# Seeding two of five accumulation banks by ScalarE in a fused attention and gate kernel

## The chip, the cores and the metric

The kernel runs on one core of a Trainium2 chip. The metric is the device time of one execution in microseconds (us), the median of several runs. Its engines are TensorE (PE, with its weight loads shown as PEld), VectorE (DVE), ScalarE (ACT), GpSimd (POOL) and SyncE (SP, which here issues loads and stores). Each engine works through its own instructions in the order in which they stand; semaphores hold an instruction back until another engine's result is there.

## The reference, cut to what matters

```python
xn = layernorm(x)                                  # x: 2048 rows of 640
q = (xn @ wq) as 32 heads of 128                   # k, v: the last 512 rows of the caches
p = softmax(q @ k.T * 128 ** -0.5)                 # for each head: 2048 x 512
s = concat(p @ v for the 32 heads) @ wo            # 2048 x 4096 times 4096 x 640
g = silu(relu(xn @ w1 + b1) ** 2 @ w2 + b2)        # 640 -> 1728 -> 640
return x + s * g
```

The output projection `@ wo` sums over all 32 heads. That running sum is what the change touches.

## The kernel before, in words

**Precision.** All products are float32. Each operand is split into a high part, which TensorE's float32r format holds, and the rest; `triple` (L560) then makes three products, high by high, high by low, low by high, into one PSUM bank. So one logical 128x128 by 128x512 product is three PE matmuls and three weight loads.

**Stages.** A first stage (to about 315 us of the trace) normalizes the rows and computes the gate for three of the four 512-row tiles. The attention stage follows and takes nearly all the rest; a short tail computes the last tile's gate and the final products.

**Units.** The attention stage is cut into 128 units (L540): two halves of the rows, in each half 16 groups of two heads, in each group two row tiles of 512, for each tile the two heads. Unit i is one head on one row tile. Each unit gets a period of nominally 12.4 us in a plan that is written out by hand (`at`, `on`, the loop from L1050): every step has a due time, the steps are sorted by it, and each engine gets its instructions in that order. The due times fix only the order.

**One unit's steps**, spread over several periods: `q_mm` (15 matmuls into a PSUM bank), `q_hi` on ACT and `q_lo` on DVE split the result and empty the bank; `s_mm` makes the scores in four banks (12 matmuls); `max_fold` on DVE takes maxima (4 instructions, tile `rdm`), `gather` on ACT and `row` on DVE finish them, and two DMAs spread them over the partitions; `shift` on DVE (4 instructions, tile `e`), `expo`, `p_hi` on ACT and `p_lo`, `s_add` on POOL make the weights; `s_fold` on DVE, `gather` on ACT (tile `rds`) and `row` sum them; `v_mm` multiplies by v (12 matmuls, tile `o`); `o_norm` on DVE, `o_hi` on ACT, `o_lo` on DVE scale and split the result (tile `ot`). `prep` splits the next heads' weights: a copy on ACT (tiles `wq`, `wk`, `wv`, `wo`) and a subtraction on POOL, two such pairs in most periods.

**The output projection.** After each second unit (odd i) the two heads' results are multiplied by their rows of `wo`, for five blocks d = 0 to 4 of 128 output columns: `r_mm` (L739), six matmuls a block, into bank `r`. `r_acc` (L753) then adds the bank to the running sum `ACC` (tile `acc`, in SBUF): in a half's first group (g == 0) ACT copies the bank there, in all later groups DVE adds it with one `tensor_tensor`.

**The two banks.** The tags `qr0` and `qr1` (`bank`, L566) are shared by `q_mm` (always `qr1`) and the five blocks (`R_BANK`, L1049: blocks 0 and 3 in `qr1`; 1, 2 and 4 in `qr0`). A bank's next user waits until the last one has been read out.

**The order on PE.** By `R_AT` (L1038), for a pair of odd unit i: in the period of an odd unit p, PE runs the scores of p (12), the second half of block 2 of unit p-4 (3), the queries of p+2 (15), **block 4 of unit p-4** (6), the products with v of p-1 (12), **block 0 of unit p-2** (6). In an even unit's period it runs scores (12), block 1 (6), queries (15), the first half of block 2 (3), v (12) and block 3 (6). So each pair of periods has 108 matmuls and all five blocks once.

**Instruction placement.** `align` (L1035) fills PE's instruction stream with no-operations up to fixed places, so that each period's instructions start at a multiple of 128. Between the last scores and the next period stand 42 matmuls with their 42 weight loads, from place 42 on, which leaves two places.

Of the kernel before, what the change touches and what calls it, by code (L numbers as in the profile page):

```python
# [10 lines left out]
AF = mybir.ActivationFunctionType  # L11
# [14 lines left out]
def kernel(  # L26
# [42 lines left out]
    class Ordered:  # L69
# [13 lines left out]
    pe, dve, act, pool, sp = (  # L83
        Ordered(e) for e in (nc.tensor, nc.vector, nc.scalar, nc.gpsimd, nc.sync)
    )
# [8 lines left out]
    def raw(ap):  # L94
        return ap.bitcast(F32)
# [387 lines left out]
    def mlp_step(n):  # L483
# [56 lines left out]
    units = [  # L540
        (hf, g, t, g * G + j)
        for hf in range(HALF)
        for g in range(NG)
        for t in range(TPH)
        for j in range(G)
    ]
    NU = len(units)
    UPG = TPH * G
    PERIOD = 12.4
    B32 = 32  # L550
    AHEAD = 2
    NQ = NT // B32
    NH = KC // 2

    XT, ACC, KT, VV, WQ, WO, Q, E, SC, MB, RD, PT, PO, OT, RB, QPS, FX, CL, PRS, RAW = (
        {} for _ in range(20)
    )
    pools = {}

    def triple(ps, a, b, start, stop):  # L560
        (ah, al), (bh, bl) = a, b
        pe.matmul(ps, ah, bh, start=start, stop=False)
        pe.matmul(ps, ah, bl, start=False, stop=False)
        pe.matmul(ps, al, bh, start=False, stop=stop)

    def bank(name, k):  # L566
        return pools["psa"].tile([P, NT], F32, tag=f"qr{k}", name=name, bufs=1)
# [19 lines left out]
    def pair(tag, shape, name, bufs):  # L587
        return [
            pools["ep"].tile(shape, F32R, tag=f"{tag}{i}", name=f"{name}_{i}", bufs=bufs)
            for i in range(2)  # L590
        ]
# [17 lines left out]
    def q_mm(i, cs):  # L609
        hf, g, t, h = units[i]  # L610
        if 0 in cs:
            QPS[i] = bank(f"pq{i}", 1)
        ws, xs = WQ[hf, h], XT[hf, t]
        for c in cs:
            triple(
                QPS[i],
                (ws[0][:, c, :], ws[1][:, c, :]),
                (xs[0][:, c, :], xs[1][:, c, :]),
                c == 0,
                c == DC - 1,  # L620
            )

    def q_hi(i):
        Q[i] = pair("q", [P, NT], f"q{i}", AHEAD + 1)
        act.activation(Q[i][0], QPS[i], AF.Copy, scale=SCALE)
# [6 lines left out]
    def s_mm(i, c):  # L632
        hf, g, t, h = units[i]
        SC[i, c] = pools["psb"].tile([P, NT], F32, tag="s", name=f"s{i}_{c}", bufs=KC)
        ks = KT[hf, h]
        cs = slice(c * P, (c + 1) * P)
        triple(SC[i, c], (ks[0][:, cs], ks[1][:, cs]), Q[i], True, True)

    def fold_tile(what, i):
        n = KC if what == "m" else 2  # L640
        return ap.tile([P, NQ, P // B32, n], F32, tag=f"rd{what}", name=f"rd{what}{i}", bufs=2)

# [16 lines left out]
    def row(i, what):  # L659
        rd = RD.pop((i, what))[:B32].rearrange("p b a c -> p b (a c)")  # L660
        r = ap.tile([B32, B32], F32, tag="row", name=f"row{what}{i}", bufs=4)
        if what == "m":
            r = r[:, :NQ]
            dve.tensor_reduce(r, rd, axis=AX.X, op=ALU.max)
        else:
            sq = SQ[i % len(SQ)]
            dve.tensor_reduce(sq[:, :NQ], rd, axis=AX.X, op=ALU.add)
            dve.reciprocal(sq[:, :NQ], sq[:, :NQ])
            dve.transpose(r, sq)
            r = r[:NQ]  # L670
        d = dpool.tile(list(r.shape), F32, tag=f"{what}_d", name=f"{what}_d{i}", bufs=4)
# [40 lines left out]
    def v_mm(i, c):  # L712
        hf, g, t, h = units[i]
        if c == 0:
            if i % 2 or i < UPG:
                PO[i] = pools["psb"].tile([P, NT], F32, tag="o", name=f"o{i}", bufs=1)
            else:
                PO[i] = psx.tile([P, NT], F32, tag="x", name=f"o{i}")
        vs, pts = VV[hf, h], PT[i, c // 2]
        triple(  # L720
            PO[i],
            (vs[0][:, c, :], vs[1][:, c, :]),
            (pts[0][:, c % 2, :], pts[1][:, c % 2, :]),
            c == 0,
            c == KC - 1,
        )
# [9 lines left out]
    def o_lo(i):  # L736
        dve.tensor_tensor(OT[i][1], PO.pop(i), raw(OT[i][0]), op=ALU.subtract)

    def r_mm(i, d, js, k):  # L739
        hf, g, t, h = units[i]  # L740
        if 0 in js:
            PRS[i, d] = bank(f"r{i}_{d}", k)
        for j in js:
            w = WO[hf, h - G + 1 + j]
            triple(
                PRS[i, d],
                tuple(x[:, d * P : (d + 1) * P] for x in w),
                tuple(OT[i - G + 1 + j]),
                j == 0,
                j == G - 1,  # L750
            )

    def r_acc(i, d):  # L753
        hf, g, t, h = units[i]
        pr = PRS.pop((i, d))
        if g == 0:
            if d == 0:
                ACC[hf, t] = keep.tile(
                    [P, DC, NT], F32, tag="acc", name=f"acc{hf}_{t}", bufs=TPH
                )  # L760
            act.activation(ACC[hf, t][:, d, :], pr, AF.Copy)
        else:
            a = ACC[hf, t][:, d, :]
            dve.tensor_tensor(a, pr, a, op=ALU.add)
# [139 lines left out]
    def late_split(f):  # L904
        n = chunks[f][1]
        r = LR.pop(f)
        kind, bufs = ("wk", G) if f % 2 else ("q", AHEAD + 1)
        if n < P:
# [93 lines left out]
    def at(when, f, *a):  # L1002
        plan.append((max(when, 0.0), len(plan), f, a))

    for n in range(HALF * NG):
        hf, g = divmod(n, NG)
        base = UPG * PERIOD * n
        for j in range(G):
            h = g * G + j
            for kind, when in (  # L1010
                ("q", (j - 1 - AHEAD) * PERIOD + (8.42 if j else 8.35)),
                ("k", (j - 2) * PERIOD + (8.5 if j else 8.37)),
# [36 lines left out]
    R_BANK, R_BANK_END = (1, 0, 0, 1, 0), (1, 1, 1, 0, 0)  # L1049
    for i in range(NU):  # L1050
        t0 = i * PERIOD

        def on(when, f, *a):
            at(t0 + when, f, *a)

        hf, g, t, h = units[i]
        for c in range(KC):
            on(0.68 * c, align, i, SLOTS[c])
            on(0.68 * c, s_mm, i, c)
        on(0.68 * KC - 0.6, align, i, SLOTS[KC])  # L1060
        qs = [(i + AHEAD, 3.45 if i % G and i > UPG else 4.3, 4.1)]
        if i == 0:
            qs = [(1, 2.8, 4.1), (2, 9.1, PERIOD - 5.2)]
        elif i < UPG:
            qs = [(i + 2, 4.9 if i == 3 else 4.2, 4.1)]
        for n, q_at, low in qs if i + AHEAD < NU else ():
            for c in range(DC):
                on(q_at + 0.68 * c, q_mm, n, (c,))
            on(q_at + 3.5, q_hi, n)
            on(q_at + low, q_lo, n)  # L1070
        for c in range(KC):
            on(0.8 + 0.68 * c, max_fold, i, c)
        on(3.95, gather, i, "m")
        on(4.1, row, i, "m")
        for c in range(KC):
            on(10.4 + 0.4 * c, shift, i, c)
        on(11.7, expo, i, 0)
        on(12.7, p_hi, i, 0)
        on(13.8, expo, i, 1)
        on(PERIOD + 4.0, p_hi, i, 1)  # L1080
        on(13.9, p_lo, i, 0)
        on(16.2, s_add, i)
        on(PERIOD + 6.2, s_fold, i)
        on(PERIOD + 8.0, gather, i, "s")
        on(PERIOD + 8.5, row, i, "s")
        on(18.6, p_lo, i, 1)
        for c in range(KC):
            on(PERIOD + 8.5 + 0.68 * c, v_mm, i, c)
        on(2 * PERIOD + 4.2, o_norm, i)
        on(2 * PERIOD + 4.9, o_hi, i)  # L1090
        on(2 * PERIOD + 5.5, o_lo, i)
        if i % G == G - 1:
            for d in range(DC):
                last = i == NU - G - 1
                if i < NU - 1:
                    for when, js in (R_AT_END if last else R_AT)[d]:
                        on(when, r_mm, i, d, js, (R_BANK_END if last else R_BANK)[d])
                    on(when + 0.68 * len(js), r_acc, i, d)
                if g == NG - 1 and hf == 0:
                    at((i + (3, 4, 5, 4, 5)[d] + (t and d in (0, 3, 4))) * PERIOD + 4.3, store_acc, t, d)  # L1100
                    w = (NU // 2 + 9 + 4 * (t * DC + d)) * PERIOD
                    for k, n in enumerate("sxg"):
                        at(w + k * PERIOD - 0.6, load_finish, n, 0, t, d)
                    at(w + 3 * PERIOD - 0.7, finish_gate, 0, t, d)
                    at(w + 3 * PERIOD - 0.7, finish, 0, t, d)
# [49 lines left out]
    for f, u in sorted(UP_AT.items()):  # L1155
        at(LOAD.get(f, PREP.get(f - 2, 0) + 0.9), late_load, 1, f)
        when = PREP.setdefault(f, u - 5.0)
# [85 lines left out]
```

## Time and profile before

| what | value |
| --- | --- |
| median of 3 runs | 1958.74 us (1958.74 to 1959.13) |
| span of the profiled execution, first to last instruction | 1956.9 us |
| PE busy | 1949.2 us, 8612 matmuls |
| DVE busy | 1537.3 us |
| POOL busy | 1376.7 us |
| ACT busy | 1187.6 us |

The profile is of one execution. Its span leaves out what lies around the instructions: the median of the timed runs is 1.8 us more. A timeline row reads: start in us from the span's start, the time that the group took, engine, source line, operation, out<-in by the program's names, shape, number of instructions that were merged into the row, and in brackets the engine's idle time before it with what ended it. Nearly all attention instructions carry line 77, because a helper there issues them; they are told apart by their tiles. `r` is a block of the output projection, `acc` the running sum, `pq` the queries' bank, `s` the scores, `o` the products with v.

### The profile page before, as it was taken

How to read it: one execution, taken by the hardware profiler on the slowest of the kernel's cores; microseconds unless marked ns; L12 is line 12 of the kernel's file. 1: busy time of each engine (PE TensorE's matmuls, PEld its weight loads, DVE VectorE, ACT ScalarE, POOL GpSimd, SP SyncE). 2: the span in 40 equal slices, each digit the busy share in tenths (PEclk: the TensorE clock that was granted, in tenths of full speed). 3: DMA queues.
4: the chain of work that ended last, by engine and by line, in shares of the span. 5: the costliest groups of instructions: out<-in, count | busy, mean ns of one | idle time of the engine just before them, and what ended most of it. 6: DMA issues, size and time to landing. Idle time of an engine off the chain costs nothing.

```text
span 1956.9 us, 28182 instructions
## 1 busy us (share of the span) xinstructions
PE 1949.2 (100%) x8612; PEld 1612.5 (82%) x8612; DVE 1537.3 (79%) x2638; ACT 1187.6 (61%) x2040; POOL 1376.7 (70%) x757
## 2 busy tenths in 40 slices
PE   9999999999999999999999999999999999999998
PEld 7888888888888888888888888888888888888887
DVE  6523337788888888888888878888888888888865
ACT  5432336766666666666666676666666666666643
POOL 2121226888888888888888888888888888888841
PEclk9999999999999999999999999999999999999999
DMA  6330454333333332332335434433333333332353
GB/s 189 88 119 28 185 198 130 97 94 92 93 92 93 92 92 92 92 92 93 93 91 179 141 117 109 114 114 114 114 113 114 113 114 114 98 92 92 85 189 118
DMA packets 127892, 219.13 MB, mean 112 GB/s; under 512 B 23452, under 2 KB 38086, under 8 KB 126470
## 3 DMA queue, kind: packets, MB, share of 16 engines
q1 hardware_dynamic: 124742, 202.75, 34.3%
q0 software_dynamic: 2864, 14.42, 1.8%
q8 instruction: 77, 1.26, 0.2%
q14 instruction: 65, 0.53, 0.1%
q10 hardware_dynamic: 144, 0.16, 0.0%
HBM read 193.41 MB, written 23.87 MB: 111 GB/s over the span
## 4 chain that ended last, share of the span: by engine, by line
PE 99%; DVE 0%; DMA 0%; ACT 0%; issue 0%; POOL 0%; POOLq 0%
PE pq L77 22%; PE r L77 22%; PE o L77 18%; PE s L77 18%; PE ph L431 7%; PE ly L77 2%; PE py L101 2%; PE py L100 2%; PE py L102 2%; PE lu L77 2%; PE eu L77 1%; PE ph L398 0%; PE py L454 0%; PE py L453 0%; DMA xb<-in_x_dram 0%; PE px L77 0%
## 5 line engine op out<-in xcount | busy, mean ns | idle before, releaser
L77 POOL TENSOR_TENSOR pt<-e,pt 128x1024 fp32r<-128x1024 f32 x256 | 615.8, 2405 | 113.6 <-ACT pt L77 68.2
L77 PE MATMUL r<-ot,wo 128*128 128x512 f32 x1920 | 496.6, 389 | 0.0
L77 PE MATMUL pq<-ax,wq 128*128 128x512 f32 x1920 | 456.1, 389 | 0.0
L77 PEld LDWEIGHTS pq<-ax,wq 128*128 128x128 f32 x1920 | 360.4, 188 | 75.2 <-DVE q L77 0.4
L77 PEld LDWEIGHTS r<-ot,wo 128*128 128x128 f32 x1920 | 360.5, 188 | 74.8
L77 PE MATMUL o<-pt,wv 128*128 128x512 f32 x1536 | 369.2, 389 | 0.0
L77 PE MATMUL s<-q,wk 128*128 128x512 f32 x1536 | 369.0, 389 | 0.0
L77 DVE TRANSPOSE_TENSOR_REDUCE rdm<-s 128x16 f32<-128x512 f32 x512 | 347.6, 712 | 6.0 <-PE s L77 5.8
L77 ACT ACTIVATE e<-e 128x1024 f32<-128x1024 f32 x256 | 269.8, 1054 | 123.8 <-DVE e L77 80.5
L77 PEld LDWEIGHTS o<-pt,wv 128*128 128x128 f32 x1536 | 288.3, 188 | 60.1 <-POOL pt L77 0.4
L77 PEld LDWEIGHTS s<-q,wk 128*128 128x128 f32 x1536 | 288.4, 188 | 59.8
L77 DVE TENSOR_TENSOR e<-s,bm 128x512 f32<-128x512 f32 x512 | 312.3, 665 | 5.8 <-DMA bm<-m_d 5.4
L77 POOL TENSOR_TENSOR su<-e,e 128x1024 f32<-128x1024 f32 x128 | 309.2, 2415 | 0.0
L77 ACT ACTIVATE pt<-e 128x1024 fp32r<-128x1024 f32 x256 | 271.9, 1062 | 6.9
L77 DVE TENSOR_TENSOR acc<-r,acc 128x512 f32<-128x512 f32 x300 | 203.6, 679 | 12.7 <-PE r L77 12.4
L77 ACT ACTIVATE rdm<-rdm 32x64 f32<-32x64 f32 x384 | 97.7, 254 | 182.1 <-DVE rdm L77 179.0
L77 DVE TRANSPOSE_TENSOR_REDUCE rds<-su 128x32 f32<-128x1024 f32 x128 | 158.4, 1237 | 0.3 <-POOL su L77 0.3
L77 DVE TENSOR_TENSOR ot<-o,ot 128x512 fp32r<-128x512 f32 x128 | 88.5, 692 | 86.1 <-ACT ot L77 86.1
L77 ACT ACTIVATE q<-pq 128x512 fp32r<-128x512 f32 x128 | 76.7, 599 | 113.6 <-PE pq L77 113.6
L431 PE MATMUL ph<-xT,w1s 128*128 128x512 f32 x585 | 139.0, 389 | 0.0
L431 PEld LDWEIGHTS ph<-xT,w1s 128*128 128x128 f32 x585 | 109.7, 188 | 22.8
L77 ACT ACTIVATE rds<-rds 32x32 f32<-32x32 f32 x384 | 89.7, 234 | 60.1 <-DVE rds L77 56.6
(137 smaller groups left out, 1942.3 us busy)
## 6 DMA issues: line engine op xcount, KB each, us to landing
bm<-m_d SPq DMA_DIRECT2D x128, 256.0 KB, 3.2
bs<-s_d SPq DMA_DIRECT2D x128, 256.0 KB, 4.0
qr<-in_wq_dram SPq DMA_DIRECT2D x64, 320.0 KB, 4.5
or<-in_wo_dram SPq DMA_DIRECT2D x64, 320.0 KB, 4.7
kr<-in_kT_dram SPq DMA_DIRECT2D x64, 256.0 KB, 4.3
vr<-in_v_dram SPq DMA_DIRECT2D x64, 256.0 KB, 4.3
xT_d<-xT POOLq DMA_DIRECT2D x6, 1280.0 KB, 7.6
ax<-xT_d SPq DMA_DIRECT2D x4, 1280.0 KB, 11.3
```

What stands on the lines that cost most here:

```text
L77: ins = method(*args, **kwargs)
L100: nc.tensor.matmul(ps, ah, bh, start=first and i == 0, stop=False)
L101: nc.tensor.matmul(ps, ah, bl, start=False, stop=False)
L102: nc.tensor.matmul(ps, al, bh, start=False, stop=last and i == n - 1)
L431: nc.tensor.matmul(ph, w1s[f][i][:, c, :], xs[j][:, c, :], start=k == 0, stop=k == len(order) - 1,)
```

## The change

In every group but a half's first, blocks 0 and 4 (`SEEDED`) no longer go through DVE's addition. Instead ACT copies the running sum into the PSUM bank ahead of the block's products (`r_seed`); the first product no longer clears the bank (`start` is false), so that the six matmuls add onto the copy; and ACT copies the finished sum back to `acc`. The last pair's blocks (units from 124 on) are left as they were. The seed is planned 0.8 us ahead of the first product, the copy back 0.2 us later than the addition was.

```diff
+    SEEDED = (0, 4)
...
-    def triple(ps, a, b, start, stop):
+    def triple(ps, a, b, start, stop, **how):
...
+    def seeded(i, d):
+
+        return units[i][1] > 0 and d in SEEDED and i < NU - UPG
+
+    def r_seed(i, d, k):
+        hf, g, t, h = units[i]
+        PRS[i, d] = bank(f"r{i}_{d}", k)
+        act.activation(PRS[i, d], ACC[hf, t][:, d, :], AF.Copy)
+
     def r_mm(i, d, js, k):
         hf, g, t, h = units[i]
-        if 0 in js:
+        if 0 in js and not seeded(i, d):
             PRS[i, d] = bank(f"r{i}_{d}", k)
...
-                j == 0,
+                j == 0 and not seeded(i, d),
                 j == G - 1,
+                skip_group_check=seeded(i, d),
...
+            act.activation(ACC[hf, t][:, d, :], pr, AF.Copy)
+        elif seeded(i, d):
             act.activation(ACC[hf, t][:, d, :], pr, AF.Copy)
         else:
             a = ACC[hf, t][:, d, :]
             dve.tensor_tensor(a, pr, a, op=ALU.add)
...
                     for when, js in (R_AT_END if last else R_AT)[d]:
-                        on(when, r_mm, i, d, js, (R_BANK_END if last else R_BANK)[d])
-                    on(when + 0.68 * len(js), r_acc, i, d)
+                        k = (R_BANK_END if last else R_BANK)[d]
+                        if seeded(i, d) and 0 in js:
+                            on(when - 0.8, r_seed, i, d, k)
+                        on(when, r_mm, i, d, js, k)
+                    on(when + 0.68 * len(js) + (0.2 if seeded(i, d) else 0.0), r_acc, i, d)
```

What it does to the instructions, engine by engine: 58 odd units (5 to 63 and 69 to 123) are seeded, so DVE loses 116 additions, and ACT gains 116 copies into PSUM and 116 copies out of it. Apart from these, each engine's instructions stand in the order of before. PE has the same matmuls; the first of blocks 0 and 4 now wait for ACT, and 30 more instructions that only wait stand in its stream. ACT's order in an odd period becomes: `ot`, **seed of block 4**, `q`, three `rds`, two weight copies, **copy back of block 4**, **seed of block 0**, `expo`, `p_hi`, **copy back of block 0**, the second `expo`.

More of the change, by code (lines that the diff above doesn't have):

```diff
@@ L558 @@
     pools = {}
-    def triple(ps, a, b, start, stop):
+    def triple(ps, a, b, start, stop, **how):
         (ah, al), (bh, bl) = a, b
-        pe.matmul(ps, ah, bh, start=start, stop=False)
-        pe.matmul(ps, ah, bl, start=False, stop=False)
-        pe.matmul(ps, al, bh, start=False, stop=stop)
+        pe.matmul(ps, ah, bh, start=start, stop=False, **how)
+        pe.matmul(ps, ah, bl, start=False, stop=False, **how)
+        pe.matmul(ps, al, bh, start=False, stop=stop, **how)
     def bank(name, k):
```

## The prediction

> **What bounds the kernel now.** I read the page first: busy shares, then the chain that ended last.
>
> ```profile
> span 1956.9 us, 28182 instructions
> ...
> PE 1949.2 (100%) x8612; PEld 1612.5 (82%) x8612; DVE 1537.3 (79%) x2638; ACT 1187.6 (61%) x2040; POOL 1376.7 (70%) x757
> ...
> PE 99%; DVE 0%; DMA 0%; ACT 0%; issue 0%; POOL 0%; POOLq 0%
> ```
>
> The chain is PE from end to end. A busy PE alone proves little, since its spans overlap; so I took the windows view of two periods from the middle of the attention stage (one odd, one even unit).
>
> ```profile
> 854.73:879.21 24.48, 24.48 (x110) 20.28 (x108) 21.54 (x38) 16.12 (x28) 19.95 (x11) 1.00 0.30 92
> ```
>
> The columns are PE, PEld, DVE, ACT, POOL, then the clock. 24.48 us for 108 matmuls (PE's 110 counts two cut at the edges) is 0.2267 us each. PE's timeline says the same:
>
> ```profile
> 848.15 2.88 PE L77 MATMUL s<-q,wk 128*128 128x512 f32 x12
> ...
> 854.95 1.52 PE L77 MATMUL r<-ot,wo 128*128 128x512 f32 x6
> ...
> 859.03 1.52 PE L77 MATMUL r<-ot,wo 128*128 128x512 f32 x6
> 860.39 2.88 PE L77 MATMUL s<-q,wk 128*128 128x512 f32 x12
> ```
>
> Twelve matmuls take 2.88 us of which the last one's own span is 0.389, so eleven steps of 0.2265: no step is longer than another. PE never waits here, it has no step to gain, and every wait that is added and not covered is paid in full. The question is whether ACT delivers the seeds in time.
>
> **When PE wants them.** The weight load, not the matmul, carries the wait. In the timeline of all engines:
>
> ```profile
> 854.73 1.32 PEld L77 LDWEIGHTS r<-ot,wo 128*128 128x128 f32 x6
> ...
> 858.81 1.32 PEld L77 LDWEIGHTS r<-ot,wo 128*128 128x128 f32 x6
> ```
>
> In this odd period block 4's first load is due at 854.73, block 0's at 858.81.
>
> **What ACT does until then**, and what each of its starts waits for:
>
> ```profile
> 851.83 0.79 ACT L77 ACTIVATE rdm<-rdm 32x64 f32<-32x64 f32 x3 [1.36 <-DVE rdm L77]
> ...
> 853.69 0.60 ACT L77 ACTIVATE ot<-o 128x512 fp32r<-128x512 f32 x1
> 855.15 0.60 ACT L77 ACTIVATE q<-pq 128x512 fp32r<-128x512 f32 x1 [0.86 <-PE pq L77]
> 856.20 0.72 ACT L77 ACTIVATE rds<-rds 32x32 f32<-32x32 f32 x3 [0.45 <-DVE rds L77]
> 856.94 0.74 ACT L77 ACTIVATE wq<-qr 128x640 fp32r<-128x640 f32 x1
> 857.59 0.62 ACT L77 ACTIVATE wv<-vr 128x512 fp32r<-128x512 f32 x1
> 859.29 1.06 ACT L77 ACTIVATE e<-e 128x1024 f32<-128x1024 f32 x1 [1.08 <-DVE e L77]
> ...
> 864.06 0.79 ACT L77 ACTIVATE rdm<-rdm 32x64 f32<-32x64 f32 x3 [1.67 <-DVE rdm L77]
> ```
>
> There are two holes: 0.86 us ahead of `q`, where block 4's seed goes, and 1.08 us ahead of `e`, where block 4's copy back and block 0's seed both go. A share of 61% for ACT looks like room, but the second hole opens only at 858.21, and PE wants its result at 858.81.
>
> **Price of a seed.** No ACT copy from SBUF to PSUM is in this trace. The nearest rows are the copies out of PSUM (tile view of `acc`: minimum, median, maximum) and the copies within SBUF:
>
> ```profile
> L77 ACT ACTIVATE acc<-r x20: 572/584/599, 346.9 to 1175.6; 128x512 f32<-128x512 f32 x20
> ...
> L77 DVE TENSOR_TENSOR acc<-r,acc x300: 636/676/692, 395.6 to 1892.3; 128x512 f32<-128x512 f32 x150
> ```
>
> ```profile
> L77 ACT ACTIVATE wk<-kr 128x512 fp32r<-128x512 f32 x64 | 39.9, 624 | 0.7
> ```
>
> So 0.57 to 0.62 us; I take 0.58, the row with one side in PSUM, and allow 0.10 to either side because the write side is untried. Copies in a queue overlap, as the first group shows, where ACT already does the copy back between two weight copies:
>
> ```profile
> 368.55 0.58 ACT L77 ACTIVATE acc<-r 128x512 f32<-128x512 f32 x1
> 369.03 0.62 ACT L77 ACTIVATE wv<-vr 128x512 fp32r<-128x512 f32 x1
> ```
>
> The next one starts 0.48 us after a copy of 0.58: 0.10 less than its span.
>
> **Price of a late seed.** The trace has two places in the attention stage's start where PE's weight load waits for another engine:
>
> ```profile
> 313.87 0.65 DVE L77 SCALAR_TENSOR_TENSOR q<-pq,q 128x512 fp32r<-128x512 f32 x1
> ```
>
> ```profile
> 314.57 0.77 PEld L77 LDWEIGHTS pq<-ax,wq 128*128 128x128 f32 x4 [0.45 <-DVE q L77]
> ```
>
> ```profile
> 314.57 3.74 PE L77 MATMUL pq<-ax,wq 128*128 128x512 f32 x15
> ```
>
> ```profile
> 343.68 0.99 PEld L77 LDWEIGHTS o<-pt,wv 128*128 128x128 f32 x5 [0.37 <-POOL pt L77]
> ```
>
> ```profile
> 342.89 2.22 PE L77 MATMUL o<-pt,wv 128*128 128x512 f32 x8
> ```
>
> DVE's result was there at 314.52 and the load started at 314.57, so the signal takes 0.05 us. A load of 0.188 us (the page's mean) in a step of 0.227 leaves 0.04 idle ordinarily, so these two came 0.41 and 0.33 us late. The second run of eight matmuls took 2.22 us against 7 x 0.2267 + 0.389 = 1.98: 0.24 lost. In the first, fifteen took 3.74 against 3.56, and they began 0.19 late (load to matmul is 0.22 ordinarily, none here): 0.36 to 0.37 lost. So PE loses the lateness less 0.05 to 0.09; I take 0.06.
>
> The Trainium skill (TensorE: Matmul & The Clock Gate, the table of specifications at its head) says that PE's queue pulls weight loads ahead of matmuls in flight; taken widely, that would hide a short wait. By that rule, the trace agrees only for the 0.06 above: both loads that waited held up what stood behind them.
>
> **The change, part by part.**
>
> *DVE, minus 116 additions* of 0.676 us, 78 us in all, two in each pair of periods. What does DVE being earlier start? Its timeline:
>
> ```profile
> 849.03 2.76 DVE L77 TRANSPOSE_TENSOR_REDUCE rdm<-s 128x16 f32<-128x512 f32 x4
> 851.75 0.69 DVE L77 TENSOR_TENSOR acc<-r,acc 128x512 f32<-128x512 f32 x1
> 852.64 0.41 DVE L77 TENSOR_REDUCE rowm<-rdm 32x16 f32<-32x256 f32 x1 [0.20 <-ACT rdm L77]
> 852.98 0.68 DVE L77 TENSOR_TENSOR o<-o,bs 128x512 f32<-128x512 f32 x1
> 854.32 0.69 DVE L77 TENSOR_TENSOR ot<-o,ot 128x512 fp32r<-128x512 f32 x1 [0.66 <-ACT ot L77]
> 854.93 1.24 DVE L77 TRANSPOSE_TENSOR_REDUCE rds<-su 128x32 f32<-128x1024 f32 x1
> ...
> 856.66 0.67 DVE L77 TENSOR_TENSOR acc<-r,acc 128x512 f32<-128x512 f32 x1
> ...
> 857.96 2.43 DVE L77 TENSOR_TENSOR e<-s,bm 128x512 f32<-128x512 f32 x4
> 860.59 0.69 DVE L77 TENSOR_TENSOR acc<-r,acc 128x512 f32<-128x512 f32 x1 [0.20 <-PE r L77]
> 861.27 2.76 DVE L77 TRANSPOSE_TENSOR_REDUCE rdm<-s 128x16 f32<-128x512 f32 x4
> ```
>
> The additions at 856.66 (block 4) and 860.59 (block 0) go. Behind the second stand the maxima; the first scores bank is complete at 860.39 + 2 x 0.2267 + 0.389 = 861.23, and they start at 861.27 already. So they cannot move. In the odd period likewise: 848.15 + 0.84 = 848.99, start 849.03. From there to ACT's `rds` at 856.20 everything follows link by link (maxima, ACT's gather, `rowm`, `o`, ACT's `ot`, DVE's `ot`, `rds`), and no removed addition lies on that way. The addition at 856.66 stands behind `rds`; without it `e` may come up to 0.3 us sooner, which nothing late needs. The relief is worth nothing on PE.
>
> *Block 4's seed.* It follows `ot`: 853.69 + 0.60 - 0.10 = 854.19, done 854.77, seen 854.82, due 854.73: 0.09 late, 0.03 lost. Its bank was read out at 852.44 (the addition of 851.75). `q`, behind it, waits for PE until 855.15 and isn't delayed.
>
> *Block 4's copy back.* It follows `wv`: 857.59 + 0.62 - 0.09 = 858.12. PE's block is complete at 856.47 (854.95 + 1.52), so it doesn't wait. 0.48 us of ACT's queue.
>
> *Block 0's seed.* 858.12 + 0.48 = 858.60, done 859.18, seen 859.23, due 858.81 (858.84 with the 0.03 above). 0.39 late, **0.33 lost**. The bank itself isn't what decides: `q_lo` has read it by 856.74.
>
> *Behind it on ACT.* The first `expo` can start at 859.08, sooner than its 859.29 of before. Block 0's copy back stands behind `p_hi`, at about 861.1; the block is complete at 860.55 + 0.36 = 860.91, so no wait. It pushes the second `expo` from 861.35 to some 861.6 and its end to 862.7, and DVE's maxima are not there before 864.06 + 0.36: the 1.67 us of idle cover it. If that cover were gone, POOL's sum and the next weights would come later by what is missing.
>
> *PE's 30 waiting instructions* fit the two places that each period leaves, at no cost; were one too many, 255 no-operations would follow, far outside the range.
>
> *Does the loss recur?* Yes. The scores move with PE, the maxima with the scores, ACT's holes with the maxima; PE's delay gives ACT no head start in the next pair. So 58 pairs x 0.36 = 20.9 us. In the first pairs of each half ACT is later, because block 2 there still goes through ACT ahead of `ot`:
>
> ```profile
> 391.64 0.72 ACT L77 ACTIVATE rds<-rds 32x32 f32<-32x32 f32 x3 [1.00 <-DVE rds L77]
> ```
>
> 1.00 us of idle behind `q` instead of 0.45: 0.55 later, for one seeded block 0 in each half, 1.1 us. At the turn of the halves one more pair is later, by 0.78 - 0.45 = 0.33:
>
> ```profile
> 1101.33 0.72 ACT L77 ACTIVATE rds<-rds 32x32 f32<-32x32 f32 x3 [0.78 <-DVE rds L77]
> ```
>
> Sum: 20.9 + 1.1 + 0.3 = 22.3 us. The profiled span becomes 1979.2, and with the 1.8 us around it, by which the median exceeds the span, **1981.0 us**.
>
> **Rivals.**
>
> 1. *The seeds are in time* (not slower). Block 0's seed must be seen 0.36 us sooner: at 58 x 0 the time is 1958.7, within 0.2%. It decides from a seed span of about 0.2 us, or from ACT's `rds` starting at 855.84. For it: ACT has 8 us idle in each pair of periods, DVE gets 1.35 us back. Against it: the hole's opening at 858.21 is tied to the scores, as above. Chance 0.08.
> 2. *The copies don't overlap when one writes PSUM.* Then the seed starts at the end of what stands before it: 0.10 for the copy back, 0.10 for its own end as PE sees it, so 0.56 instead of 0.36 a pair: 58 x 0.56 + 1.4 = 33.9, 1993 us. Against it: all rows of ACT overlap by 0.10. Chance 0.12.
> 3. *DVE was the hidden bound.* The Trainium skill (Perfetto Trace Analysis, Optimizing Scalar/DVE Operations) says that with DVE saturated, moving work to ScalarE may make sense. DVE's 21.54 of 24.48 us is the row for it. But PE's steps are even and the maxima start 0.04 us behind the scores; all that PE waits in the attention stage is the 0.6 us above, so the most is 1958 us, inside 0.2%. For truly faster I leave 0.02.
>
> **How the numbers follow.** The forecast has 0.78, with seeds from 0.48 to 0.68 us: 0.10 x 58 = 6 us either way, 1975 to 1988. The range must leave out no more than 2 in 10: from 1972 (a seed of 0.48 whose wait PE absorbs a bit better) to 1994, which takes in rival 2. A measurement here can tell about 0.2%, 4 us. Slower by more than that: 0.90; within: 0.08; faster: 0.02.
>
> **What would show it.** After: PE's weight loads of `r` with about 0.4 us of idle time released by ACT `r`, once a pair, and hardly any ahead of block 4; the pair of periods 24.84 us long instead of 24.48; DVE's maxima still 0.04 us behind the scores; ACT's seed at 0.58 us. A seed row under 0.4 us, or maxima that start apart from the scores, would make it wrong.

## The result, and the profile after

The changed kernel takes 1981.55 us (median of 4 runs, 1981.09 to 1981.58) against 1958.74 us before: 1.0115 times as long, 95% interval 1.0101 to 1.0130, or 22.8 us more. The forecast was 1981.0 us. The profiled execution's span grew by the same 22.8 us, so its rows can be held against the total. From the page of the changed kernel:

```profile
span 1979.7 us, 28358 instructions
...
PE 1968.3 (99%) x8612; PEld 1604.4 (81%) x8612; DVE 1478.5 (75%) x2522; ACT 1299.3 (66%) x2272; POOL 1377.8 (70%) x757
...
PE 74%; DVE 16%; ACT 8%; issue 1%; DMA 0%; SPq 0%; POOL 0%; DVEq 0%; POOLq 0%
```

DVE gave up 59 us of busy time and ACT took on 112; neither number says anything about the time. The line that does is the chain: it was PE for 99% and is now handed through DVE and ACT, because PE waits. Who waits for whom on PE's weight loads (us in total, times, longest):

```profile
PEld r L77 <- ACT r L77: 33.8, 93, 1.1
```

No such row stood in the kernel before. An odd period in the middle shows both seeds. First ACT:

```profile
861.22 0.60 ACT L77 ACTIVATE ot<-o 128x512 fp32r<-128x512 f32 x1
861.72 0.60 ACT L77 ACTIVATE r<-acc 128x512 f32<-128x512 f32 x1
862.68 0.60 ACT L77 ACTIVATE q<-pq 128x512 fp32r<-128x512 f32 x1 [0.37 <-PE pq L77]
863.73 0.74 ACT L77 ACTIVATE rds<-rds 32x32 f32<-32x32 f32 x3 [0.45 <-DVE rds L77]
864.49 0.74 ACT L77 ACTIVATE wq<-qr 128x640 fp32r<-128x640 f32 x1
865.14 0.62 ACT L77 ACTIVATE wv<-vr 128x512 fp32r<-128x512 f32 x1
865.66 0.58 ACT L77 ACTIVATE acc<-r 128x512 f32<-128x512 f32 x1
866.14 0.59 ACT L77 ACTIVATE r<-acc 128x512 f32<-128x512 f32 x1
866.66 1.05 ACT L77 ACTIVATE e<-e 128x1024 f32<-128x1024 f32 x1
```

The hole behind `wv` is filled without a gap: copy back of block 4, seed of block 0, then `expo`. PE's weight loads at the same time:

```profile
858.85 3.36 PEld L77 LDWEIGHTS pq<-ax,wq 128*128 128x128 f32 x15
862.36 1.23 PEld L77 LDWEIGHTS r<-ot,wo 128*128 128x128 f32 x6
863.63 2.68 PEld L77 LDWEIGHTS o<-pt,wv 128*128 128x128 f32 x12
866.78 1.23 PEld L77 LDWEIGHTS r<-ot,wo 128*128 128x128 f32 x6 [0.47 <-ACT r L77]
868.05 2.68 PEld L77 LDWEIGHTS s<-q,wk 128*128 128x128 f32 x12
```

Block 4's first load was due at 858.85 + 15 x 0.2267 = 862.25, came at 862.36, 0.11 late; the load behind the block, due at 863.61, came at 863.63: 0.02 lost. Block 0's was due at 863.63 + 12 x 0.2267 = 866.35 and came at 866.78, 0.05 behind the seed's end at 866.73: 0.43 late. The scores behind it, due at 867.71, came at 868.05: 0.34 lost. So 0.36 us a pair, where the forecast had 0.03 and 0.33. Counted in the trace over all 58 pairs (from the first weight load of one group to that of the next, less 0.2267 us a matmul), 21.2 us were lost at block 0 and 1.1 at block 4: all but 0.5 of the 22.8. Groups of matmuls that no wait touches keep their step of 0.2267 us, as before.

### The profile page after: what moved, and what is told of

The parts are those of the page before. It is cut to its first block, busy times and chain, and to the rows that moved or that the text cites. A ratio compares the mean times of both kernels' runs of the same rounds, so it can differ in the third digit from the quotient of the medians.

```text
span 1979.7 us, 28358 instructions
## 1 busy us (share of the span) xinstructions
PE 1968.3 (99%) x8612; PEld 1604.4 (81%) x8612; DVE 1478.5 (75%) x2522; ACT 1299.3 (66%) x2272; POOL 1377.8 (70%) x757
## 4 chain that ended last, share of the span: by engine, by line
PE 74%; DVE 16%; ACT 8%; issue 1%; DMA 0%; SPq 0%; POOL 0%; DVEq 0%; POOLq 0%
PE r L77 17%; PE pq L77 14%; PE s L77 13%; PE o L77 12%; PE ph L431 7%; DVE rdm L77 6%; DVE rds L77 3%; DVE e L77 3%; PE ly L77 2%; PE py L100 2%; PE py L102 2%; PE py L101 2%; PE lu L77 2%; DVE ot L77 2%; ACT rdm L77 1%; DVE acc L77 1%
## 5 line engine op out<-in xcount | busy, mean ns | idle before, releaser
L77 PE MATMUL r<-ot,wo 128*128 128x512 f32 x1920 | 505.4, 394 | 4.0 <-ACT r L77 1.9
L77 PEld LDWEIGHTS r<-ot,wo 128*128 128x128 f32 x1920 | 351.8, 188 | 105.2 <-ACT r L77 33.8
L77 DVE TRANSPOSE_TENSOR_REDUCE rdm<-s 128x16 f32<-128x512 f32 x512 | 352.8, 718 | 80.9 <-PE s L77 80.9
L77 DVE TENSOR_TENSOR acc<-r,acc 128x512 f32<-128x512 f32 x184 | 124.5, 677 | 5.5 <-PE r L77 5.5
L431 PEld LDWEIGHTS ph<-xT,w1s 128*128 128x128 f32 x585 | 109.7, 188 | 22.8
```

Source lines behind the costliest of these rows:

```text
L77: ins = method(*args, **kwargs)
L431: nc.tensor.matmul(ph, w1s[f][i][:, c, :], xs[j][:, c, :], start=k == 0, stop=k == len(order) - 1,)
```

## The experiments

**Theory:** block 0's seed stands in ACT's queue behind two weight copies and block 4's copy back, and comes 0.4 us late; the loss is in the order of the queue. **Rival A:** a seeded block has a fixed price on PE. **Rival B:** ACT's added load slows the chain of work as such. A third question is whether DVE's relief is worth anything.

### Each part alone

Only block 4:

```diff
-    SEEDED = (0, 4)
+    SEEDED = (4,)
```

> Only block 4 is seeded and copied back by ACT; block 0 stays with DVE's addition. Theory (a queue: block 0's seed stands behind two weight copies and block 4's copy back and comes 0.4 us late): block 4's seed alone loses what it lost in the changed kernel, 0.02 us a pair, so 58 x 0.02 = 1 us: 1959 to 1961 us. Rival A (each seeded block costs PE a fixed amount, half of 22.8 us): 1970 us. Rival B (ACT's added work as such slows the chain, 116 of 232 copies): 1970 us.

Measured: 1960.53 us, 1.0008 times before (0.9999 to 1.0017), before at 1958.92. A difference of 1.6 us isn't clear of noise; this run's trace, counted as above, has 1.2 us of it at block 4. Only block 0, `SEEDED = (0,)`:

> Only block 0 is seeded and copied back by ACT; block 4 stays with DVE's addition. Theory: without block 4's copy back the seed starts 0.48 us sooner and is seen 0.06 us ahead of its load, so nothing is lost in a steady pair; what is left are the first pairs of the halves (0.88 us each, since ACT does block 4's copy there already) and about 0.5 us in the last: 1960 to 1962 us. So the two parts alone cost 1 and 2 us, and together 22.8. Rival A (a fixed price for each seed, nearly all of it block 0's): 1979 us. Rival B (ACT's load): 1970 us.

Measured: 1961.23 us, 1.0012 times before (1.0003 to 1.0021). ACT and the loads in this run:

```profile
858.89 0.61 ACT L77 ACTIVATE wv<-vr 128x512 fp32r<-128x512 f32 x1
859.41 0.58 ACT L77 ACTIVATE r<-acc 128x512 f32<-128x512 f32 x1
```

```profile
857.38 2.68 PEld L77 LDWEIGHTS o<-pt,wv 128*128 128x128 f32 x12
860.10 1.32 PEld L77 LDWEIGHTS r<-ot,wo 128*128 128x128 f32 x6
```

The seed is done at 859.99, seen at 860.04, due at 860.10: 0.06 us in hand, as worked out. One part costs 1.6 us, the other 2.3, both together 22.8. That rules out A, and B as a price of each copy: nothing that each seed or copy costs by itself adds up so. The parts collide. A load that does harm only when both parts are there is left; the next run has that load in full.

### The same instructions in another order

Block 4's copy back goes behind block 0's seed:

```diff
-                    on(when + 0.68 * len(js) + (0.2 if seeded(i, d) else 0.0), r_acc, i, d)
+                    late = (0.2 if d == 0 else 2.2) if seeded(i, d) else 0.0
+                    on(when + 0.68 * len(js) + late, r_acc, i, d)
```

> Both blocks seeded as in the change, with the same instructions; only block 4's copy back stands behind block 0's seed instead of ahead of it. Theory: the seed is seen at 858.75 against 858.81, in time; block 4's 1 us and the first pairs' 2 us stay: 1960 to 1963 us. Rivals A and B, for which the order within ACT's queue is nothing: 1981 us.

Measured: 1962.40 us, 1.0018 times before (1.0009 to 1.0026), within the theory's numbers. ACT's and PE's instructions are those of the changed kernel, one pair of copies a period pair is swapped, and 19 of the 22.8 us are gone. So the load as such is not the cause. ACT in the middle of this run, and block 0's load, due and started at 859.79:

```profile
858.56 0.62 ACT L77 ACTIVATE wv<-vr 128x512 fp32r<-128x512 f32 x1
859.08 0.58 ACT L77 ACTIVATE r<-acc 128x512 f32<-128x512 f32 x1
859.60 0.58 ACT L77 ACTIVATE acc<-r 128x512 f32<-128x512 f32 x1
```

```profile
859.79 1.32 PEld L77 LDWEIGHTS r<-ot,wo 128*128 128x128 f32 x6
```

The seed is seen at 859.71, 0.08 us ahead. The waits that stay (three of them, in the first seeded pairs of the halves and in the last, make up most):

```profile
PEld r L77 <- ACT r L77: 3.0, 5, 1.0
```

### DVE's relief alone

In the kernel before, DVE's additions of blocks 0 and 4 are left out:

```diff
-        else:
+        elif d in (1, 2, 3) or i >= NU - UPG:
             a = ACC[hf, t][:, d, :]
             dve.tensor_tensor(a, pr, a, op=ALU.add)
```

> The kernel before, with DVE's additions for blocks 0 and 4 left out in the 58 pairs that the change seeds (so these blocks' sums are missing from the output), and nothing added to ACT. It measures DVE's relief by itself. Theory: PE has no wait to lose, 1958.2 to 1958.8 us, no difference. Rival (DVE's 88% in the attention stage was a hidden bound): faster by some of the 78 us of DVE time, 1955 us or less.

Measured: 1958.68 us, 0.9998 times before (0.9989 to 1.0007). DVE's busy time is 59 us less (the 116 additions' own spans sum to 78), and nothing of it arrives. Where it went stands in this run's waits:

```profile
DVE rdm L77 <- PE s L77: 55.8, 56, 1.4
```

It became DVE's wait for the scores. In the kernel before, the same order had no idle time there, because the addition ended just when the scores came. An engine at 88%, without a gap ahead of its longest group, was not the bound.

### Seeds earlier still

Block 0's seed ahead of the weight copies:

```diff
-                            on(when - 0.8, r_seed, i, d, k)
+                            on(when - (0.8 if d else 3.05), r_seed, i, d, k)
```

> Both blocks seeded; block 0's seed stands ahead of the two weight copies (right behind the second gather, when its bank has been read) instead of behind them and the copy back. Theory: it is seen at about 857.5 against 858.81, also in the first pairs of the halves (0.8 us in hand there); only block 4's 1 us is left, and the weight copies come 0.5 us later, which POOL covers: 1959 to 1961 us. Rivals A (fixed price of a seed) and B (ACT's load): 1981 us.

Measured: 1961.71 us, 1.0016 times before (1.0007 to 1.0025), 0.7 above the expected range. Then block 4's seed early as well (`3.02 if d` in place of `0.8 if d`):

> As the run with block 0's seed early, and block 4's seed too is put ahead: before the second copy of the weights' high part and the attention output's copy, right behind the first gather. Theory: no seed is late any more, and PE is back at the kernel before: 1958.7 us, if the 0.5 us by which the attention output's copy and all behind it on ACT and DVE come later stays covered. If that isn't covered: a loss of its own, up to 0.4 us a pair, 1959 to 1980. In no case under 1958.

Measured: 1964.56 us, 1.0030 times before (1.0018 to 1.0041): worse than with one seed early. No load waits for a seed any more, but others do. The weight loads' waits for POOL, first with block 0's seed early, then with both:

```profile
PEld o L77 <- POOL pt L77: 3.2, 11, 0.3
```

```profile
PEld o L77 <- POOL pt L77: 7.2, 11, 0.7
```

One of the eleven was there before (the 0.4 us at 343.68 in the prediction). The other ten are 49 us apart, one in each four periods of the second half, where POOL also does a finishing addition for the first half's rows (tile `fs`). POOL at the same place in the kernel before, then with both seeds early, and the load that waits:

```profile
1371.86 1.57 POOL L77 TENSOR_TENSOR wo<-or,wo 128x640 fp32r<-128x640 f32 x1 [0.98 <-ACT wo L77]
```

```profile
1374.30 1.58 POOL L77 TENSOR_TENSOR wo<-or,wo 128x640 fp32r<-128x640 f32 x1 [1.93 <-ACT wo L77]
...
1377.76 1.30 POOL L77 TENSOR_TENSOR fs<-fs,fx 128x512 f32<-128x512 f32 x1 [0.63 <-ACT acc L77]
1379.01 2.41 POOL L77 TENSOR_TENSOR pt<-e,pt 128x1024 fp32r<-128x1024 f32 x1
1381.36 2.42 POOL L77 TENSOR_TENSOR su<-e,e 128x1024 f32<-128x1024 f32 x1
1383.72 2.41 POOL L77 TENSOR_TENSOR pt<-e,pt 128x1024 fp32r<-128x1024 f32 x1
```

```profile
1386.18 0.99 PEld L77 LDWEIGHTS o<-pt,wv 128*128 128x128 f32 x5 [0.72 <-POOL pt L77]
```

POOL waits 1.93 us instead of 0.98 for ACT's weight copy, which now stands behind the seeds. From 1377.76 to 1386.13 it works without a gap, and PE takes its last result at once. Counted as above, the ten pairs lose 0.55 to 0.60 us each, 5.8 us: all that this run is slower. With block 0's seed alone early they lose 0.14 to 0.20 each, 1.7 us, and with block 4's 1.1 that is nearly all that that run is slower. In all other pairs POOL's slack covers the later copies; "POOL covers" in the expectation was read from a pair that has no finishing addition. So putting both seeds as early as possible isn't the cure. For block 0's seed the place behind the weight copies, but ahead of the copy back (1962.40 us), costs about as little as the place ahead of them (1961.71).

### A larger dose

Block 0's seed twice, as a first try at doubling the delay:

```diff
-        act.activation(PRS[i, d], ACC[hf, t][:, d, :], AF.Copy)
+        for _ in range(1 if d else 2):
+            act.activation(PRS[i, d], ACC[hf, t][:, d, :], AF.Copy)
```

> The change, with block 0's seed written twice in a row (the same values). Theory: the loss grows by the second copy's place in the queue, 0.48 us if the copies overlap, 0.58 if the second waits for the first: 58 x 0.48 = 28 us to 58 x 0.58 = 34 us more, 2009 to 2016 us. Rival A (a fixed price of a seeded bank): 1981 us. Rival B (ACT's load, 58 more copies on top of 232): a quarter of 22.8 more, 1987 us.

Measured: 2546.33 us, 1.300 times before. No theory had this. The page and PE's timeline:

```profile
span 2544.3 us, 35328 instructions
```

```profile
1080.51 1.65 PE L77 MATMUL r<-ot,wo 128*128 128x512 f32 x6 [0.67 <-ACT r L77]
1099.34 5.46 PE L77 MATMUL s<-q,wk 128*128 128x512 f32 x12 [17.18 <-issue]
```

```profile
PE s L77 <- issue: 463.9, 27, 17.2
```

PE stands for 17 us ahead of the scores, 27 times, waiting for nothing that the profile shows but its own instructions. The second write of the bank adds waiting instructions to PE's stream (171 in the trace, against 113 in the changed kernel), and in 27 periods three of them now stand where two have a place. These are the 27 periods with a stall, and in them 255 no-operations stand from the last group's loads to the next scores: the filling up to the next multiple of 256. If that is so, one place more must cure it. The same kernel with the last alignment place at 41 (`SLOTS = (0, 11, 22, 33, 41)`):

> The run with block 0's seed twice, with the last alignment place of PE's stream at 41 instead of 42, which leaves three places for waiting instructions in each period instead of two (that run has 27 periods with three). Theory: its 27 stalls of 19.7 us between two units were 255 no-operations that filled the stream up to the next multiple of 256, and are gone; what stays is block 0's wait, longer by the second seed, 0.5 to 0.62 us a pair on top of the change: 2010 to 2018 us. Rival (the second write of the bank itself stops PE): 2546 us as before.

Measured: 2018.12 us, 1.0302 times before (1.0285 to 1.0319), 0.1 above the range. Its page:

```profile
span 2017.9 us, 28415 instructions
```

6913 instructions fewer, 27 x 256 and one; in the traces all of them are no-operations of PE (9361 against 2448). The 27 periods still have three waiting instructions each, and no stall. That settles the 528 us. A dose that leaves PE's instructions alone is block 4's copy back done twice:

```diff
-            act.activation(ACC[hf, t][:, d, :], pr, AF.Copy)
+            for _ in range(2 if d else 1):
+                act.activation(ACC[hf, t][:, d, :], pr, AF.Copy)
```

> The change, with block 4's copy back done twice in a row (the same values), ahead of block 0's seed. PE's instructions, its waits and its seeds are those of the change. Theory: block 0's seed comes later by the second copy's place in the queue, 0.48 us if the copies overlap, some 0.6 if the second waits for the first: 58 x 0.48 = 28 to 58 x 0.6 = 35 us more, 2009 to 2016 us. Rival A (a fixed price of a seeded bank): 1981 us. Rival B (ACT's load, 58 more copies on top of 232): 1987 us.

Measured: 2016.68 us, 1.0296 times before (1.0281 to 1.0311), 35.1 us above the changed kernel, 0.61 a pair. ACT there, and block 0's load:

```profile
876.19 0.62 ACT L77 ACTIVATE wv<-vr 128x512 fp32r<-128x512 f32 x1
876.71 1.21 ACT L77 ACTIVATE acc<-r 128x512 f32<-128x512 f32 x2
877.82 0.60 ACT L77 ACTIVATE r<-acc 128x512 f32<-128x512 f32 x1
```

```profile
878.47 1.22 PEld L77 LDWEIGHTS r<-ot,wo 128*128 128x128 f32 x6 [1.07 <-ACT r L77]
```

Two copies take 1.21 us, not 0.48 + 0.58 = 1.06: the second, which writes what the first wrote, starts only when the first is done. From the first copy back to the seed it is 1.11 us instead of 0.48, 0.63 more, and a pair loses 0.95 to 0.97 us at block 0 instead of 0.34, some 0.62 more. The first seeded pair of each half has no second copy ahead of its seed, because block 4's copy back there is still that of the half's first group, which was not doubled; it loses 0.88, as before. No seed was added on PE's side, which rules out A once more, and B, which had 1987. None of the nine versions beats the kernel before, and none could by much: PE had 0.6 us of waits to give in the attention stage.

## Why the prediction was right

- *What bounds.* PE, as read from even steps of 0.2267 us; the run without additions shows that DVE's relief was worth nothing. It was 59 us of busy time, not the 78 that the spans of the additions sum to.
- *Price of a seed.* Taken as 0.58 from the nearest row; the tile view of the changed kernel gives minimum, median and maximum:

```profile
L77 ACT ACTIVATE r<-acc x116: 581/595/600, 394.3 to 1880.6; 128x512 f32<-128x512 f32 x116
```

- *Block 0's lateness.* 0.39 was forecast, 0.43 measured; PE absorbed 0.09 of it and not 0.06, so that 0.33 came out at 0.34. Both errors are within the spread of the rows that they were taken from.
- *Block 4.* 0.03 forecast, 0.02 measured: 1.1 us over all pairs, and 1.2 in the run with block 4 alone. The forecast expected hardly any waits of its loads; the row of 93 has 35 of them beside block 0's 58, each just over 0.15 us of idle time, of which PE loses 0.02.
- *It recurs and does not grow.* The pair takes 24.84 us instead of 24.48, as forecast: the scores of one odd period start at 855.68, those of the next odd one at 880.52. DVE's maxima start when the scores come, 0.04 us behind the first bank (869.16, complete at 869.12), now with idle time ahead. PE's timeline, the windows view of that pair (the clock is third from the right) and DVE's timeline:

```profile
855.68 2.88 PE L77 MATMUL s<-q,wk 128*128 128x512 f32 x12
...
880.52 2.88 PE L77 MATMUL s<-q,wk 128*128 128x512 f32 x12
```

```profile
855.68:880.52 24.84, 24.79 (x110) 20.13 (x109) 20.37 (x36) 18.03 (x33) 19.97 (x11) 1.00 0.27 91
```

```profile
869.16 2.76 DVE L77 TRANSPOSE_TENSOR_REDUCE rdm<-s 128x16 f32<-128x512 f32 x4 [1.47 <-PE s L77]
```

- *The odd pairs.* The first pairs of the halves lost 0.89 and 0.88, as forecast (0.36 + 0.55 is 0.91). The pair at the turn, for which 0.33 was added, lost no more than any other: ACT's `rds` came there after 0.45 us, not 0.78. In the kernel before, DVE's `e` of the period ahead had waited 0.48 us for a DMA:

```profile
1091.41 2.48 DVE L77 TENSOR_TENSOR e<-s,bm 128x512 f32<-128x512 f32 x4 [0.48 <-DMA bm<-m_d]
```

The run without additions has 1.39 us of it at this place, and its `rds` comes after 1.41; the changed kernel has no such wait there. So the lateness goes with a DMA whose landing differs from execution to execution, and the term of 0.33 rested on one execution's. The last seeded pair, which had no term of its own, lost 0.96, since ACT has a third weight copy ahead of the seed there. The load:

```profile
1860.87 1.23 PEld L77 LDWEIGHTS r<-ot,wo 128*128 128x128 f32 x6 [1.08 <-ACT r L77]
```

These two errors, 0.3 too much and 0.6 too little, partly cancel in the sum: that the forecast is within 0.6 us is in part luck.
- *The rivals.* Seeds in time: they are in time as soon as the copy back stands behind (1962.40), so that case was 0.4 us of queue away. Copies that don't overlap: not here; the only plain copies in these runs that were seen not to overlap are those where one writes what the one before it wrote. The two free places in PE's stream were both taken in 28 periods and overrun in none; the aside on 255 no-operations became real with one more waiting instruction.

## What to carry to other kernels

A new wait on a saturated engine is priced by one row: what stands ahead of the producer's instruction in its own queue at that moment, not by the producer's share of busy time. Two moves that each cost next to nothing can cost much together if they use the same hole; try the order within the hole before giving up the move. Relief for a second engine is worth nothing while its instructions start at the bound engine's results, whatever its share.

## What the runs showed of the hardware

- A weight load that waits for a semaphore holds everything behind it on PE. Of a lateness of 0.43 us PE absorbed 0.09.
- After 17 us of nothing but no-operations the next 12 matmuls took 5.46 us instead of 2.88. The windows view of that stretch in the run with block 0's seed twice gives the granted clock (third number from the right):

```profile
1099.30:1104.60 5.30, 5.26 (x13) 4.18 (x14) 2.16 (x3) 0.00 (x0) 0.00 (x0) 0.50 0.01 3
```

17.2 us of standing and 2.6 us at half the clock make 19.8; the run lost 528 / 27 = 19.6 us a stall. The Trainium skill (TensorE: Matmul & The Clock Gate, the table of the two clock states) says that an idle window of about 3.4 us halves the clock. The 0.50 here agrees, but no run here tries an idle time near that length. The waits of 0.4 us in the changed kernel left the clock at 1.00.
- An ACT copy of 128x512 float32 from SBUF into PSUM took 0.595 us and one from PSUM to SBUF 0.580 (medians in the changed kernel); one within SBUF, which wrote float32r, took 0.624 (the mean in the kernel before).
- Copies in ACT's queue start 0.48 us apart, 0.10 before the end of the one ahead; a second copy that writes what the first wrote started 0.61 us after it.
